# New delays in the planner that orders the work behind attention, and a fixed place for its loads

## The chip, the core and the metric

The kernel runs on one core of one Trainium2 chip. The metric is the device time in microseconds (us); lower is better. Three runs of the kernel before gave 654.6, 655.8 and 655.89 us, so the median is 655.8 us. TensorE is called PE here, VectorE DVE, ScalarE ACT, GpSimd POOL, and SyncE SP; PEld is PE's loading of weights.

## The reference

Three layers follow one another on 1152 tokens (2 batches of 576) of 512 channels:

```python
scores = 0.125 * q @ k.T + slope[h] * -abs(i - j)      # 8 heads of 64, window of 128, causal
x = softmax(scores) @ v                                # to (1152, 512)
p = probs / (probs.sum(-1) + 1e-9)                     # 4 experts
x = sum(p[:, e:e+1] * (relu(x @ w1[e]) @ w2[e]) for e in range(4))      # w1 512x1024
xn = x / sqrt(mean(x * x) + 1e-6) * rms_g
out = (silu(xn @ w_gate) * (xn @ w_val)) @ w_out       # 512x1536 and back
```

## The kernel before, in words

Every fp32 operand of a product is split in two fp32r parts, a high part (a copy on ACT) and a low part (a subtraction on DVE), and three matmuls stand for one. The experts are taken in 8 units of half an expert (u = 0 to 7), the last layer in 3 units of 512 hidden channels. In a unit the first products (into the hidden channels) use a scheme with seven products of half-size blocks in place of eight (`products`, L1057): tokens and weights are first added and subtracted in blocks on DVE, and the seven results are joined by a chain of small steps. One call of `products` gives PE seven blocks of six matmuls each, into banks a and c or b and d by turns: pa, pb, pc and pd, and then, adding to the first ones, ka, kc and kd. Behind pa ACT copies the bank to `x`; behind pb DVE adds into `x`; behind pc it adds to the first half of `r`, behind pd again. kc may start when the first add to `r` is done, since it writes the bank which that add reads, and kd when the second is. Behind kd come two more adds, and then relu, or silu and a multiplication, into `h` (L1142, L1148, L1154). The second products (`out_plain`, L1198) go over 9 tiles of 128 tokens with 12 matmuls of 512 columns each (L1207); their left side is the split of `h` (tile `oa`, made by `plain_parts`, L1178), their right side the split of the second weights (tile `wa`).

Besides this, DVE and ACT do side work all the time: the splits and block sums of the next unit's weights (`raw` to `wb` and `wa`), and a conversion of the last layer's weights from 64-bit words (`converted`, L985: ACT at L1014, DVE at L1017, L1020, L1023, in tile `stage`), which SP stores to DRAM (L1032) and loads again later. The loads of raw weights go into a ring of two buffers (`raw`), those of 64-bit words into a ring of three (`scratch`, named t in the code), both at L865.

Attention is a list written out by hand (`ORDERS`, `Flow`). Behind it a planner sets the order, when the program is built:

- `Plan.pe` takes PE's blocks in program order and keeps PE's clock `self.t`. `Plan.now` (L138) issues a step that the products need. `Plan.later` puts side work on a list with a time by which it is due. `Plan.step` (L92) picks from the list what can start soonest, with 0.03 per us of due time added, and `now` calls it to fill the time until the needed step is ready. With `slack`, `now` takes first what is due within it.
- A step's cost is `HOLD + elements * RATE`: it holds DVE for 0.07 + n/960 us, ACT for 0.09 + n/1200, and a load of n = 512 holds the queue for 1.48. Its result counts as there `MORE` later (DVE 0.085, ACT 0.1, a load 2.0, PE 0.17). `End.seen` says when an engine may use it: `LAT` = 0.04 later on another engine, and on the same engine already when the hold ends.
- A side step is taken into the time ahead of a needed one when it ends at most 0.18 us behind it.

At the end (L1534 to L1544) each engine's instructions are tied one to the next in this order, from the first of attention on; SP's only as far as attention goes (`listed`). SP's later loads and stores are ordered by the framework's own scheduler, which may put them between attention's.

Of the kernel before, what the change touches and what calls it, by code (L numbers as in the profile page):

```python
# [42 lines left out]
class End:  # L43
# [10 lines left out]
    def seen(self, e):  # L54

        if self.of is not None:
            return max((x.seen(e) for x in self.of), default=0.0)
        return self.hold if e == self.e and e is not None else self.own + Plan.LAT


class Plan:

    LAT = 0.04
    HOLD = {"d": 0.07, "a": 0.09, "q": 0.2}
    MORE = {"d": 0.085, "a": 0.1, "q": 2.0, "t": 0.17}
    RATE = {"d": 1 / 960, "a": 1 / 1200, "q": 0.0025}

    def __init__(self, free):  # L70
# [21 lines left out]
    def step(self, until, only=None, due=None):  # L92

        found = None
        for i, job in enumerate(self.jobs):
            if due is not None and job[4] > due:
                continue
            b = self.best(job)
            if b and b[0] < until and (only is None or b[1] == only and (due is not None or b[0] + self.cost(only, job[1]) < until + 0.18)):
                key = (b[0] + 0.03 * job[4], job[4], i)  # L100
                if found is None or key < found[0]:
                    found = key, job, b[1]
        if found is None:
            return False
        _, job, e = found
        self.jobs.remove(job)
        needs = job[2]
        if job[6]:
            ring, done = job[6]
            used = min(ring, key=lambda x: x.t)  # L110
            ring.remove(used)
            ring.append(done)
            done.slot = used.slot
            needs = needs + [used]
        self.issue(e, job[1], needs, job[3], job[5])
        return True

    def issue(self, e, n, needs, emit, end):
        start = max(self.free[e], self.ready(needs, e))
        emit(e)  # L120
        self.free[e] = start + self.cost(e, n)
        end.own, end.e, end.hold = self.free[e] + self.MORE[e], e, self.free[e]

# [29 lines left out]
    def pe(self, n, cols, needs, emit):  # L153
# [4 lines left out]
        self.t = start + n * (cols / 2400 + 0.013)  # L158
        return End(self.t + self.MORE["t"], "t", self.t)


class Flow:
# [4 lines left out]
    FORM = {"s": "s", "o": "o", "z": "o", "x": "x"}  # L167
    LAT = {"t": 0.055, "d": 0.036, "a": 0.036, "p": 0.17, "q": 0.1}

# [10 lines left out]
    def run(self, orders, shared):  # L180
# [14 lines left out]
        while any(rows.values()):  # L195
            heads = [(e, r[0]) for e, r in rows.items() if r and all(n in done for n in self.ops[r[0]][3])]
            for e, i in heads:
                kind, _, costs, needs, _ = self.ops[i]
                t = max([self.free[e]] + [done[n] + self.LAT[e] for n in needs if at[n] != e or e == "q"])
                if e == "t":  # L200
# [35 lines left out]
def tile_fused(ctx: ExitStack, tc: tile.TileContext, qS, kS, vS, probs, w1, w2, wgv, wo, g, out):  # L236
# [123 lines left out]
    with (  # L360
# [37 lines left out]
        mark = len(tc.nc.cur_bb.bb.instructions)  # L398
# [354 lines left out]
        prev = dict.fromkeys("sxowf")  # L753
# [31 lines left out]
        listed = len(tc.nc.cur_bb.bb.instructions)  # L785
# [4 lines left out]
    more_slot = End(0.0)  # L790
# [8 lines left out]
    pl = Plan(flow.free)  # L799
# [3 lines left out]
    coming, gates, outs = [], [], []  # L803
# [38 lines left out]
    class Issued:  # L842
# [5 lines left out]
        @property  # L848
        def t(self):
            return self.end.t - Plan.MORE["q"] - pl.LAT  # L850

        def seen(self, e):
            return self.end.t - Plan.MORE["q"]

# [87 lines left out]
    def load_one(src, due, slots=None):  # L942

        slots = slots or [take("wa") for _ in range(4)]
        return load_unit(*src, 0, slots, slots, due)
# [232 lines left out]
    def plain_parts(t, due):  # L1178

        na, da = take("oa")  # L1180

        def w(p):
            return na.slot[:, p, :].rearrange("p (k m) -> p k m", k=4)

        gs = groups(t, t + 1)
        src = h[:, :, t * P : (t + 1) * P]
        end = parts_of(512, w, lambda: src, [na] + [written[g] for g in gs], due)
        for g in gs:
            reading[g].append(end)
        copied[t] = end  # L1190
        return w, end, da
# [24 lines left out]
    def out_tiles(w, put, parts, ahead, between=lambda t: None, last=(), width=DM, tiles=(0, NTT), begun={}):  # L1216

        for t in range(*tiles):
            for i in range(t, min(t + ahead + 1, tiles[1])):
                if i not in parts:  # L1220
                    parts[i] = plain_parts(i, pl.t + 2.7 * (i - t))
            end = t == NTT - 1
            out_plain(parts.pop(t), w, t, put, last if end else (), width if end else DM, t > tiles[1] - 3, begun.get(t))
            between(t)
# [47 lines left out]
    units = [f(20 + 10 * i) for i, f in enumerate(load_w1(*W1[1]))]  # L1272
    right = [first, token_sums(1, End(0.0), w1_read, 28)[0]]
    rewrite(1)
    for t0 in (S, S + HT):
# [5 lines left out]
        if t0 == S:  # L1281
            parts = {t: plain_parts(t, pl.t + 2 + t - 4) for t in (4, 5)}
# [121 lines left out]
    for u in range(1, NU):  # L1404
        w, w_read = nxt
        now_units, units = units, []
        parts = {}
        last = u == NU - 1

        def put(t, c, src, needs, u=u):  # L1410
            return mix(u, t, c, src, needs)

        if last:
            hg = pl.later("q", 256, [], lambda e: nc.sync.dma_start(out=g_cols, in_=g.rearrange("(k p) -> p k", p=P)), pl.t)
        for i, gr in ((0, 0), (1, 0), (0, 1), (1, 1)):
            hidden_products(now_units[i], right[gr], i, gr)
            if (i, gr) == (0, 1) and not last:
                more = load_w1(*W1[u + 1])
                units.append(more[0](pl.t + 20))
            elif (i, gr) == (0, 1):  # L1420
                more = load_w1(*gates[1:3])
                units.append(more[0](pl.t + 18))
                out_tiles(w, put, parts, 1, finish, tiles=(0, 4))
            if (u, i, gr) == (1, 0, 1):
                store_next(3, pl.t)
            if (i, gr) == (1, 0):
                if last:
                    pl.later("a", 1500, [], lambda e: nc.scalar.activation(out=rstd, in_=ident[:, :NTT], func=AF.Sqrt), pl.t)
                for t in range(2 if last else 3):
                    parts[t] = plain_parts(t, pl.t + 6 + 2 * t)  # L1430
        if not last:
            units.append(more[1](pl.t + 20))
            nxt = load_w2(W2[u + 1], pl.t + 30)
            store_next(STORES[u], pl.t + 24)
            spare = KEEP * (u == NU - 2)
            out_tiles(w, put, parts, 3, last=w_read, tiles=(0, NTT - spare))
            kept = [(t, parts.get(t) or plain_parts(t, pl.t)) for t in range(NTT - spare, NTT)], w, w_read
            if u == NU - 2:
                lent = [take("t") for _ in range(RINGS["t"])]
                for x, done in lent:  # L1440
                    i = thirds.index(x.slot)
                    x.slot = late(lambda i=i: third(i, [P, 2, 512], F32R))
                    done.slot = late(lambda i=i: third(i, [P, 1024], F32))
                first_units = [load_one(gates[0], pl.t + 20, [*lent, (more_slot, End())])]
            continue
        first_units += units
        first_units.append(more[1](pl.t + 18))
        begun, tags = {}, (("a", "c"), ("b", "d"))[(turn["pr"] + 1) % 2]
        for i in range(4, TA):
            parts[i] = plain_parts(i, pl.t - 4)  # L1450
        for n, (t, x) in enumerate(kept[0]):
            begun[t] = out_first(x, kept[1], tags[n // 2], kept[2] if t == NTT - 1 else ())
            if n == 1:
                transposes(pl.t + 6, 0, 1, 2, 3)
                out_tiles(w, put, parts, 0, finish, tiles=(4, TA))
        units = [load_one(gates[3], pl.t + 20)]

        def between(t):
            finish(t)
            if t == NTT - KEEP:  # L1460
                transposes(pl.t + 2, *range(4, TA))
                sums.append(exact_sums(0, pl.t + 2.72 * (NTT - 1 - t)))

        sums = []
        out_tiles(w, put, parts, 2, between, w_read, tiles=(TA, NTT), begun=begun)
# [12 lines left out]
    units = [f(start + 52 + 6 * i) for i, f in enumerate(pair)]  # L1478
# [20 lines left out]
    for u in range(NV):  # L1499
        if u == 0:  # L1500
            right, parts = first_unit()
            pl.slack = None
        else:
            parts = {}
# [28 lines left out]
    traced = tc.nc.cur_bb.bb.instructions  # L1533
    ET = mybir.EngineType  # L1534
    for e in (ET.PE, ET.DVE, ET.Activation, ET.Pool, ET.SP):
        prev = None
        for i in traced[mark : listed if e == ET.SP else None]:
            if i.engine == e:
                if prev is not None:
                    tc.add_manual_dep(  # L1540
                        i, prev.name, mybir.DependencyInfo(mybir.DependencyClass.NoSync, mybir.DependencyReason.DATA),
                        reason="order",
                    )
                prev = i  # L1544


# [30 lines left out]
```

## Time and profile before

| | |
|---|---|
| median of 3 runs (lowest to highest) | 655.8 us (654.6 to 655.89) |
| the profiled execution: its time | 654.55 us |
| its span, first to last instruction | 652.8 us |
| granted TensorE clock over the span | 1.00 |
| PE, DVE, ACT, POOL busy in the span | 642.2, 512.7, 323.2, 43.4 us |
| instructions of PE (matmuls) | 4226 |

The span is the time on the core; the 1.75 us between it and the execution's own time lie around it. Busy PE time counts matmuls that overlap, so it hides short stops: a stop is read from the distance between the starts of two matmuls. Attention takes the first 82 us, with the first expert's products filled in, the experts go on to 442 us, and the last layer takes the rest.

### The profile page before, as it was taken

To read this page: it belongs to the slowest core of one execution; us is meant where nothing else is said; L and a number is where in the kernel's file an instruction comes from. 1 tells how busy PE (TensorE), PEld (TensorE's weight loads), DVE (VectorE), ACT (ScalarE), POOL (GpSimd) and SP (SyncE) were. 2 spreads that over 40 slices of the span, in tenths; PEclk is the share of its full clock that TensorE was granted. 3 is DMA by queue.
4 is the path that set the end of the run, shared out by engine and by line. 5 is a ranking of instruction groups with operands and counts; after the bars stand their busy time and mean duration, and the time that the engine had idled before them with its cause. 6 is when DMAs were issued, how large, how long until landed. Compare 5 with 4: busy or idle time off the path is not lost.

```text
span 652.8 us, 11281 instructions
## 1 busy us (share of the span) xinstructions
PE 642.2 (98%) x4226; PEld 579.2 (89%) x4226; DVE 512.7 (79%) x1167; ACT 323.2 (50%) x756; POOL 43.4 (7%) x94
## 2 busy tenths in 40 slices
PE   6999998999999999999999999999999999999998
PEld 5688797989989989989889898889998999899986
DVE  6988676697786987987978988798989488838573
ACT  6988464543542642633534456676446334303230
POOL 6764100000000000000000000000000000000000
PEclk9999999999999999999999999999999999999999
DMA  8542014056133635545435231101314300101012
GB/s 280 179 143 66 1 34 135 26 178 188 57 97 129 194 97 154 169 125 150 144 130 175 79 102 50 33 32 66 101 63 162 114 30 35 34 2 40 27 49 96
DMA packets 24758, 64.71 MB, mean 99 GB/s; under 512 B 3200, under 2 KB 6272, under 8 KB 24704
## 3 DMA queue, kind: packets, MB, share of 16 engines
q1 hardware_dynamic: 24416, 63.70, 30.7%
q8 instruction: 33, 0.54, 0.3%
q10 hardware_dynamic: 288, 0.30, 0.1%
q14 instruction: 21, 0.17, 0.1%
HBM read 52.19 MB, written 11.80 MB: 98 GB/s over the span
## 4 chain that ended last, share of the span: by engine, by line
PE 88%; DVE 6%; ACT 2%; DMA 2%; issue 1%; SPq 0%; DVEq 0%
PE ps_c L1075 12%; PE ps_a L1207 12%; PE ps_d L1075 11%; PE ps_b L1207 9%; PE ps_a L1075 8%; PE ps_b L1075 8%; PE ps_d L1207 8%; PE ps_c L1207 7%; PE a L673 2%; PE pst L570 2%; PE po L589 2%; PE a L704 2%; PE s L503 2%; DVE wb L821 1%; DVE r L824 1%
## 5 line engine op out<-in xcount | busy, mean ns | idle before, releaser
L1207 PE MATMUL ps_a<-wa,oa 128*128 128x512 f32 (+1 forms) x372 | 85.0, 382 | 0.0
L1207 PEld LDWEIGHTS ps_a<-wa,oa 128*128 128x128 f32 x372 | 68.3, 188 | 13.6
L828 ACT ACTIVATE wb<-raw 128x512 fp32r<-128x512 f32 (+1 forms) x99 | 50.3, 531 | 50.6 <-DVE raw L821 46.1
L821 DVE TENSOR_TENSOR oa<-h,oa 128x512 fp32r<-128x512 f32 x95 | 64.0, 683 | 2.3 <-ACT oa L828 2.0
L1207 PE MATMUL ps_b<-wa,oa 128*128 128x512 f32 x276 | 65.0, 390 | 0.0
L828 ACT ACTIVATE oa<-h 128x512 fp32r<-128x512 f32 x95 | 56.0, 619 | 8.7 <-DVE h L1154 4.5
L1207 PEld LDWEIGHTS ps_b<-wa,oa 128*128 128x128 f32 x276 | 51.2, 188 | 10.2
L1207 PE MATMUL ps_d<-wa,oa 128*128 128x512 f32 x240 | 56.2, 389 | 0.0
L821 DVE TENSOR_TENSOR wb<-raw,wb 128x512 fp32r<-128x512 f32 (+1 forms) x99 | 54.2, 566 | 0.1
L1207 PEld LDWEIGHTS ps_d<-wa,oa 128*128 128x128 f32 x240 | 45.0, 188 | 9.3
L1207 PE MATMUL ps_c<-wa,oa 128*128 128x512 f32 x216 | 50.7, 389 | 0.0
L828 ACT ACTIVATE wa<-raw 128x512 fp32r<-128x512 f32 (+1 forms) x55 | 30.3, 590 | 38.1 <-DMA raw<-in_w 26.4
L1207 PEld LDWEIGHTS ps_c<-wa,oa 128*128 128x128 f32 x216 | 40.5, 188 | 8.3
L1075 PE MATMUL ps_d<-xh,wb 128*128 128x288 f32 (+2 forms) x176 | 43.5, 300 | 2.1 <-DVE r L824 2.1
L821 DVE TENSOR_TENSOR wa<-raw,wa 128x512 fp32r<-128x512 f32 (+1 forms) x55 | 34.1, 642 | 13.7 <-ACT wa L828 13.7
L1075 PE MATMUL ps_b<-xh,wb 128*128 128x288 f32 (+2 forms) x176 | 43.0, 298 | 0.0
L1075 PE MATMUL ps_c<-xh,wb 128*128 128x288 f32 (+2 forms) x176 | 41.8, 295 | 0.0
L1075 PE MATMUL ps_a<-xh,wb 128*128 128x288 f32 (+2 forms) x176 | 41.1, 291 | 0.0
L1142 ACT ACTIVATE h<-r 128x576 f32<-128x576 f32 x28 | 19.2, 686 | 40.0 <-DVE r L824 40.0
L824 DVE TENSOR_TENSOR r<-ps_c,x 128x288 f32<-128x288 f32 (+2 forms) x52 | 23.2, 446 | 16.6 <-PE ps_c L1075 13.8
L828 ACT ACTIVATE x<-ps_b 128x288 f32<-128x288 f32 (+2 forms) x26 | 10.6, 408 | 47.5 <-PE ps_b L1075 47.4
L821 DVE TENSOR_TENSOR raw<-raw 128x256 f32<-128x256 f32 x78 | 32.9, 422 | 1.5
(290 smaller groups left out, 1559.4 us busy)
## 6 DMA issues: line engine op xcount, KB each, us to landing
raw<-in_w SPq DMA_DIRECT2D x32, 512.0 KB, 3.8
scratch<-in_wgv SPq DMA_DIRECT2D x24, 512.0 KB, 4.6
f<-stage SPq DMA_DIRECT2D x36, 256.0 KB, 2.6
raw<-f SPq DMA_DIRECT2D x18, 512.0 KB, 3.3
scratch<-in_wo SPq DMA_DIRECT2D x12, 512.0 KB, 4.6
vt<-in_vS SPq DMA_DIRECT2D x4, 512.0 KB, 6.3
out_y<-acc SPq DMA_DIRECT2D x8, 256.0 KB, 2.0
qt<-in_qS SPq DMA_DIRECT2D x7, 288.0 KB, 4.2
```

The costliest lines, as they stand in the source:

```text
L503: nc.tensor.matmul(sps[n, t][o : o + D, :], lhsT=qts[n][rows, t * D : (t + 1) * D], rhs=kts[n][rows, k0:k1], start=True, stop=True,)
L570: nc.tensor.transpose(pst[:w, j, :], tts[n % 2][:, 2 * kb + j, c0 : c0 + w], ident)
L589: nc.tensor.matmul(po[r, kb * P : kb * P + len(range(blocks.shape[1])) * P], lhsT=vt[:, kb, v], rhs=blocks[:, :, 1:3, :] if j else blocks[ ...
L673: nc.tensor.matmul(box[0], lhsT=a, rhs=x[:, k, tok], start=k == 0 and a is wh and x is xh, stop=k == 3 and a is wl)
L704: nc.tensor.matmul(box[0], lhsT=tile[0][:, x, k, :], rhs=v[:, i, :], start=k == 0 and x == i == 0, stop=k == 3 and x == 1)
L821: EN[e].tensor_tensor(out=out, in0=a, in1=b, op=ALU.subtract)
L824: EN[e].tensor_tensor(out=out, in0=a, in1=b, op=ALU.add)
L828: nc.scalar.activation(out=out, in_=a, func=AF.Copy)
L1075: nc.tensor.matmul(ps, lhsT=s[:, k, :], rhs=t(k), start=start and m == 0, stop=m == 5, skip_group_check=True,)
L1142: return wrote(gr, pl.now("a", tok.stop - tok.start, needs + was_reading[gr], lambda e: nc.scalar.activation(out=h[:, c, tok], in_=src, fu ...
L1207: nc.tensor.matmul(ps[:, :width], lhsT=a(s)[:, k, :], rhs=w[k][0]()[:, i, c], start=not (n or begun), stop=(n == 11))
```

## The change

The times of the planner change, some due times with them, and the tie of SP's instructions. Nothing that is computed changes.

```diff
     def seen(self, e):
-        return self.hold if e == self.e and e is not None else self.own + Plan.LAT
+        return self.own + (Plan.LAT if e != "t" else 0.0 if self.e == "t" else Plan.PELAT)
 class Plan:
-    LAT = 0.04
+    LAT, PELAT = 0.08, 0.15
     HOLD = {"d": 0.07, "a": 0.09, "q": 0.2}
-    MORE = {"d": 0.085, "a": 0.1, "q": 2.0, "t": 0.17}
+    MORE = {"d": 0.085, "a": 0.1, "q": 3.0, "t": 0.17}
...
-            if b and ... (due is not None or b[0] + self.cost(only, job[1]) < until + 0.18)):
+            if b and ... (due is not None or b[0] + self.cost(only, job[1]) < until + 0.0)):
...
     def out_tiles(...):
-                    parts[i] = plain_parts(i, pl.t + 2.7 * (i - t))
+                    parts[i] = plain_parts(i, pl.t + 2.7 * (i - t) - 4)
...
                 more = load_w1(*gates[1:3])
-                units.append(more[0](pl.t + 18))
+                units.append(more[0](pl.t + 30))
...
-                first_units = [load_one(gates[0], pl.t + 20, [*lent, (more_slot, End())])]
+                first_units = [load_one(gates[0], pl.t + 50, [*lent, (more_slot, End())])]
...
-        first_units.append(more[1](pl.t + 18))
+        first_units.append(more[1](pl.t + 30))
...
     for e in (ET.PE, ET.DVE, ET.Activation, ET.Pool, ET.SP):
         prev = None
-        for i in traced[mark : listed if e == ET.SP else None]:
+        for n, i in enumerate(traced[mark:], mark):
             if i.engine == e:
                 if prev is not None:
                     tc.add_manual_dep(i, prev.name, ...)
-                prev = i
+                if e != ET.SP or n < listed:
+                    prev = i
```

In words: a result counts for any engine, its own too, only when it is wholly written, plus 0.08 us (plus 0.15 for PE, which keeps its own order). A load is taken to land 3.0 us behind its hold, not 2.0. A side step must end before the needed step can start. The splits of `h` for a second product are due 4 us earlier, the first two weight units of the last layer later. And each of SP's instructions behind attention comes behind attention's last one.

## Rows read from the trace of the kernel before

**Rows 1.** Windows: us, busy time of PE, PEld, DVE, ACT, POOL, clock, DMA share, GB/s

```profile
100.00:125.00 25.00, 23.23 (x158) 22.06 (x158) 14.61 (x30) 10.99 (x22) 0.00 (x0) 1.00 0.32 104
425.00:500.00 75.00, 74.61 (x477) 69.31 (x476) 68.88 (x148) 44.83 (x99) 0.00 (x0) 1.00 0.25 83
```

**Rows 2.** Timeline of PE at 109 us: start, us, what, idle before

```profile
109.08 0.29 PE L1075 MATMUL ps_b<-xh,wb 128*128 128x288 f32 x1
111.15 0.40 PE L1075 MATMUL ps_d<-xh,wb 128*128 128x288 f32 x1 [1.77 <-DVE r L824]
111.39 0.30 PE L1075 MATMUL ps_d<-xl,wb 128*128 128x288 f32 x1
```

**Rows 3.** Chain that ended last, from 100 to 112 us

```profile
103.85 5.50 DMA raw<-in_w
```

**Rows 4.** Timeline of DVE, 104 to 113 us

```profile
107.13 0.46 DVE L824 TENSOR_TENSOR x<-ps_b,x 128x288 f32<-128x288 f32 x1 [2.10 <-PE ps_b L1075]
110.03 0.69 DVE L821 TENSOR_TENSOR wa<-raw,wa 128x512 fp32r<-128x512 f32 x1 [2.45 <-ACT wa L828]
110.64 0.45 DVE L824 TENSOR_TENSOR r<-ps_d,x 128x288 f32<-128x288 f32 x1
```

**Rows 5.** Timeline of PE at 221 and at 363 us

```profile
221.25 0.29 PE L1075 MATMUL ps_a<-xl,wb 128*128 128x288 f32 x1
221.38 0.29 PE L1075 MATMUL ps_a<-xh,wb 128*128 128x288 f32 x1
221.66 0.40 PE L1075 MATMUL ps_c<-xh,wb 128*128 128x288 f32 x1
221.90 0.29 PE L1075 MATMUL ps_c<-xl,wb 128*128 128x288 f32 x1
...
222.43 0.29 PE L1075 MATMUL ps_c<-xh,wb 128*128 128x288 f32 x1
222.63 0.66 PE L1075 MATMUL ps_c<-t,wb 128*128 128x288 f32 x3
...
363.16 0.40 PE L1075 MATMUL ps_c<-xh,wb 128*128 128x288 f32 x1
```

**Rows 6.** Timeline of DVE, 216 to 222 us

```profile
218.67 0.45 DVE L824 TENSOR_TENSOR r<-ps_d,x 128x288 f32<-128x288 f32 x1
...
220.59 0.45 DVE L824 TENSOR_TENSOR x<-ps_a,x 128x288 f32<-128x288 f32 x1
221.15 0.46 DVE L824 TENSOR_TENSOR r<-ps_c,x 128x288 f32<-128x288 f32 x1
221.52 0.68 DVE L1023 SCALAR_TENSOR_TENSOR stage<-scratch,stage 128x512 int32<-128x512 int32 x1
222.12 0.45 DVE L824 TENSOR_TENSOR r<-ps_c,r 128x288 f32<-128x288 f32 x1
```

**Rows 7.** Timeline of PE at 457 and at 601 us

```profile
456.93 0.31 PE L1075 MATMUL ps_b<-xh,wb 128*128 128x320 f32 x1
457.53 0.41 PE L1075 MATMUL ps_d<-xh,wb 128*128 128x320 f32 x1 [0.30 <-DVE r L824]
...
600.62 0.28 PE L1075 MATMUL ps_a<-xh,wa 128*128 128x256 f32 x1
601.05 0.39 PE L1075 MATMUL ps_c<-xh,wa 128*128 128x256 f32 x1
```

**Rows 8.** Timeline of SP, the first 40 us

```profile
3.66 0.56 SPq L865 DMA_DIRECT2D scratch<-in_wgv  x1
...
6.90 0.43 SPq L1414 DMA_DIRECT2D g_cols<-in_g  x1
...
37.05 0.51 SPq L430 DMA_DIRECT2D vt<-in_vS  x1
```

**Rows 9.** Everything that PE waited for (us, times, longest)

```profile
...
PE ps_d L1075 <- DVE r L824: 2.1, 2, 1.8
PE s L503 <- DMA kt<-in_kS: 1.7, 1, 1.7
```

More of the change, by code (lines that the diff above doesn't have):

```diff
@@ L98, in step @@
             b = self.best(job)
-            if b and b[0] < until and (only is None or b[1] == only and (due is not None or b[0] + self.cost(only, job[1]) < until + 0.18)):
+            if b and b[0] < until and (only is None or b[1] == only and (due is not None or b[0] + self.cost(only, job[1]) < until + 0.0)):
                 key = (b[0] + 0.03 * job[4], job[4], i)
```

## The prediction

> **What bounds the kernel now.** I read the page's busy times first: PE is at work in 642.2 of 652.8 us, so no other engine can set the time except by stopping PE. The windows say where to look: from 100 to 125 us PE lacks 1.8 us, and from 425 to 500 us it lacks 0.4, while DVE there works 68.88 of 75 us and has 6.1 us to spare [rows 1]. Busy time hides short stops, since matmuls overlap, so I then went through PE's timeline and looked only at the distance between starts. Undisturbed, matmuls of 288 columns start 0.13 us apart from 221.25 to 221.38 [rows 5]. What is longer is a stop:
>
> - At 109 us PE starts 2.07 us after the matmul before, and the next one 0.24 later. Less 0.13 each time that is 1.94 + 0.11 = 2.05 us [rows 2].
> - At 221.66, 0.28 less 0.13, and 0.24 less 0.13 behind it; at 222.63 0.20 less 0.13, and three matmuls there take 0.66 where 2 x 0.13 + 0.29 = 0.55 would do. That is 0.15 + 0.11 + 0.07 + 0.11 = 0.44 us. It returns in each of four units of the experts, 4 in all, the last at 363.16: 1.76 us [rows 5].
> - At 457.53, 0.60 against 0.15 (320 columns), and at 601.05, 0.43 against 0.12 (256 columns) [rows 7]: 0.45 and 0.31, each with the 0.11 behind it that every stop has: 0.98 us.
>
> Together that is 4.8 us; smaller ones are left out. Everything else behind attention is matmul after matmul. So this change, which leaves PE's work alone, can win some 4.8 us there and hardly more.
>
> What ends each stop? PE waits for the adds into `r` [rows 2, 7, 9]. At 109 us a load issued at 103.85 took 5.50 us to land [rows 3]. ACT's copy for `wa` waited for it, DVE's subtraction for `wa` waited at 110.03 for the copy, and the add into `r`, which PE needs, stood in DVE's queue behind the subtraction until 110.64 [rows 4]. Its own inputs were there long before: pc's matmuls ended 12 matmuls ahead of 109.08, at about 107.5, and the add into `x` had started at 107.13. At 221 us nothing is loaded: a chain of adds, `x` at 220.59, `r` at 221.15, `r` at 222.12 with a conversion step at 221.52 put between, is simply later than planned [rows 6].
>
> **The planner's clock against the trace.** The add at 220.59 lasts 0.45 us and the one that needs its result starts 0.56 behind it; the step at 221.52, which needs nothing of it, follows after only 0.37 [rows 6]. The old plan gives both 0.07 + 288/960 = 0.37. The new one keeps 0.37 for the independent step and plans 0.37 + 0.085 + 0.08 = 0.535 for the dependent one, within 0.03 of the trace. For PE behind a DVE add the trace has 221.66 - 221.15 = 0.51, plus the 0.11 that follows, 0.62; the old plan says 0.37 + 0.085 + 0.04 = 0.495, the new one 0.37 + 0.085 + 0.15 = 0.605. For the load, old 1.48 + 2.0 = 3.48, new 4.48, trace 5.50 [rows 3]. So each new number moves toward the rows and none passes them. One rule speaks against it: the Trainium skill, VectorE: DVE Perf Modes, section The DRAIN you can't avoid, says that the next DVE step never starts before the pipe is empty, so that a dependence costs nothing on top; by it the extra 0.165 is fiction. Rows 6 go against that rule here, with 0.37 and 0.56; what it would give is a rival below.
>
> **The change part by part.**
>
> Loads at 3.0: the planned landing moves 1.0 us later, with two latencies 0.08 more. The old plan put the subtraction for `wa` ahead of an add that could start at about 107.9 (a latency after pc's end), so it expected it before then; 1.08 us later it falls behind that add, and most likely behind the second add too, which could start some 0.8 us after the first (one block of six matmuls, 6 x 0.13). The copy still stands in ACT's queue and waits, but behind it is only relu's copy of a bank that PE needs a product later. Bounds for this term: 2.05 when both adds go ahead, 1.0 when only the wait gets shorter. I take **2.05**, since the first add alone lets PE's kc go on and the second needs only 0.8 us.
>
> Dependent steps at full length, and no side step that overruns: in the chain of rows 6 the step at 221.52 would have to end before the add at 222.12 can start. Each link is worth 0.165 to 0.2 of lateness, and 0.18 was the permitted overrun; a stop of 0.44 is about two links. Which side step comes there in the new order can't be read from the rows, so I take three of the four stops as gone, **1.3 us**; bounds 0 and 1.76.
>
> The same at 457 and 601 us, where DVE is 92% busy (68.88 of 75) around the first [rows 1]: half, **0.5 us**; bounds 0 and 0.98.
>
> Due times: splits of `h` 4 us earlier, two weight units 12 us later, one 30 later. No row shows a wait for either, so nothing is gained; the cost, if a split now pushes a needed step, is one stop like those at 221 us, **0.44 us**, bounds 0 and the slower rival.
>
> SP's order: two loads leave the start, words for `scratch` at 3.66 and `g_cols` at 6.90, and go behind 37.05 [rows 8]. They are moved past attention's loads of q, k, v and the first weights. PE's one wait for a load in attention is for `kt` [rows 9], which is ahead of both in the queue; so I cost it at nothing. The cover is that attention waits for DVE, not for loads; if it is gone the other way, the loads behind them come sooner, at most that one wait of 1.7 us, which I don't count. DVE, ACT and PE keep attention's order, since the planner starts behind it.
>
> **The sum:** 2.05 + 1.3 + 0.5 - 0.44 = 3.4 us. The profiled execution of 654.55 us would become 651.15; it lies 1.25 under the median, so against the median of 655.8 the forecast is **652.4 us**.
>
> **The rivals.**
>
> Only the load's term: a dependent step costs no more than any other (the page's rule), or the stops at 221 us come from work that must be done there. Then the reordering moves nothing else: 655.8 - 2.05 = 653.75. For it: that term alone rests on a plain error of the plan; against it, 0.37 and 0.56. Chance 0.14, of which 0.04 for the rule.
>
> No change: every order is new, and the stops come back elsewhere, since a load can still take 5.50 where 4.48 is planned: 655.8. Chance 0.13.
>
> Slower: late weights in the last layer. Side steps are refused that would not wholly fit, and their dependents are held longer, so DVE leaves holes. Around 425 to 500 us it has 6.1 us left [rows 1]. Once the refused work there exceeds this, weights whose due time was moved back are not split when a unit of the last layer begins, and PE waits. The nearest price is its one wait for a late load, 2.05 us [rows 2]; at the start of each of three units that is 6.15, against 2.05 + 1.3 won elsewhere: 655.8 + 2.8 = 658.6. Against it: the chip already pays these latencies, so the holes exist today and the same work fits. Chance 0.11.
>
> **How the numbers follow.** The forecast has 0.62. Within it the terms' bounds run from all 4.8 us gone, 651.0, to little more than the load's. The low end goes 0.8 lower, to 650.2, for the smaller stops and because one run before lay 1.2 under the median. The high end, 656.2, takes in the case without change and leaves out the slower one. About 0.2% (1.3 us) is what a measurement of this kernel tells from no change. The forecast and the load's term alone both lie under it: 0.76 faster. Same is 0.13, slower 0.11.
>
> **What would show it.** In the profile after: no stop of 2 us near 109, and the add into `r` ahead of the `wa` subtraction there; four starts fewer or shorter at the third block of the experts' late products; starts of dependent adds still 0.56 apart; `scratch` and `g_cols` behind the last `vt`; attention's end unmoved. I am wrong if PE shows new stops, above all with a wait for `wb` or `wa` at a unit's start in the last layer, or if DVE's busy time there falls while weights come late.

## The result, and the profile after

The changed kernel takes 648.06 us (median of 4 runs, 647.76 to 648.33) against 655.68 us (4 runs, 654.6 to 655.89): a ratio of 0.9887, 95% interval 0.987 to 0.9904. That is 7.6 us faster, more than twice the 3.4 us forecast, and below the range given (650.2 to 656.2).

| | before | after |
|---|---|---|
| profiled execution: time | 654.55 | 647.98 |
| its span | 652.8 | 646.2 |
| PE's stops behind 80 us, added up | 6.87 | 2.16 |
| start of PE's scores for the third pair of heads | 12.56 | 10.72 |

The third line is worked out from PE's timeline: for any two matmuls in sequence from 80 us on, the distance between their starts less (columns/2400 + 0.013) us, all added. In each kernel 1.2 us of it is no stop but the 36 transposes, which are that much longer.

So the 6.57 us between the two profiled executions have two parts: 4.7 us of stops behind attention are gone, and in attention PE starts the third pair of heads 1.84 us sooner, a lead that stays the same up to 100 us. The medians differ by 1.1 us more. Of 50 further runs of the kernel before, made beside the experiments below, 19 had a granted clock of 1.000 over the span, as its profiled execution and all four runs of after had (median 654.42 us), and 29 had 0.997 (median 655.88); what that is stands in the last section.

First the windows of after that answer to [rows 1]; the columns are the same.

```profile
100.00:125.00 25.00, 25.00 (x179) 24.40 (x178) 16.72 (x35) 13.13 (x27) 0.00 (x0) 1.00 0.31 106
425.00:500.00 75.00, 74.92 (x479) 69.76 (x478) 69.39 (x147) 46.22 (x102) 0.00 (x0) 1.00 0.27 94
```

PE now works all of the first window, and DVE in the second does 0.5 us more, not less (the same stretch of time, by then 5 to 6 us further on in the work): no sign of the holes that the slower rival feared from refused side steps.

PE's timeline at the place of [rows 2], and DVE's for [rows 4]:

```profile
107.25 0.29 PE L1075 MATMUL ps_b<-xh,wb 128*128 128x288 f32 x1
107.38 0.29 PE L1075 MATMUL ps_d<-xh,wb 128*128 128x288 f32 x1
107.51 0.30 PE L1075 MATMUL ps_d<-xl,wb 128*128 128x288 f32 x1
```

```profile
105.29 0.46 DVE L824 TENSOR_TENSOR x<-ps_b,x 128x288 f32<-128x288 f32 x1 [1.08 <-PE ps_b L1075]
105.99 0.46 DVE L824 TENSOR_TENSOR r<-ps_d,x 128x288 f32<-128x288 f32 x1 [0.24 <-PE ps_d L1075]
106.79 0.46 DVE L824 TENSOR_TENSOR r<-ps_d,r 128x288 f32<-128x288 f32 x1 [0.34 <-PE ps_d L1075]
109.15 0.69 DVE L821 TENSOR_TENSOR wa<-raw,wa 128x512 fp32r<-128x512 f32 x1 [1.90 <-ACT wa L828]
```

Both adds into `r` now stand ahead of the subtraction for `wa`. The load still lands late (the subtraction waits 1.90 us for the copy of it), but no add that PE needs stands behind it. The one larger stop of after lies at 441 us, where before has none, 0.39 less 0.15 and then 0.26 less 0.15:

```profile
440.94 0.31 PE L1075 MATMUL ps_a<-xh,wb 128*128 128x320 f32 x1
...
441.33 0.42 PE L1075 MATMUL ps_a<-th,wb 128*128 128x320 f32 x1
441.59 0.31 PE L1075 MATMUL ps_a<-tl,wb 128*128 128x320 f32 x1
```

Now the start, which I had costed at nothing. SP's queue of after, which answers to [rows 8]: the words and `g_cols` come behind the last `vt`, as the diff says.

```profile
35.21 0.73 SPq L430 DMA_DIRECT2D vt<-in_vS  x1
35.98 0.58 SPq L865 DMA_DIRECT2D scratch<-in_wgv  x1
36.61 0.54 SPq L1414 DMA_DIRECT2D g_cols<-in_g  x1
```

PE's start with the third pair and the DVE step of that time, of the kernel before and then of after:

```profile
12.03 0.16 DVE L546 TENSOR_SCALAR st<-st 128x3 f32<-128x3 f32 x1
...
12.56 0.34 PE L503 MATMUL s<-kt,qt 64*64 64x64 f32 x4 [2.21 <-DVE st L546]
```

```profile
11.93 0.16 DVE L546 TENSOR_SCALAR st<-st 128x3 f32<-128x3 f32 x1
...
10.72 0.50 PE L503 MATMUL s<-kt,qt 64*64 64x64 f32 x10 [0.56 <-DMA kt<-in_kS]
```

The profile of before names DVE's step as what PE waited for. In after the same step runs at nearly the same time, 11.93, and PE starts 1.2 us ahead of it. So PE never needed that step; what it waited for was the load of `kt`. The name is an inference, the last of several semaphores to rise, and it was wrong here. The time from issue to landing says the same. In before this `kt` is issued at 6.42, behind the words, and takes 6.0 us (line 424 from 6.3 to 6.8 us), so it lands at 12.43; after's chain of work has it at 6.54 with 4.05 us, landing at 10.59. In both PE starts 0.13 us behind the landing.

```profile
DMA to landing us min/median/max: 6.0/6.0/6.0
```

```profile
6.54 4.05 DMA kt<-in_kS
```

Of the 1.84 us, 0.50 are there one pair earlier, at the second pair's scores, before and then after:

```profile
7.72 0.82 PE L503 MATMUL s<-kt,qt 64*64 64x64 f32 x18 [1.72 <-DMA kt<-in_kS]
```

```profile
7.22 0.82 PE L503 MATMUL s<-kt,qt 64*64 64x64 f32 x18 [1.18 <-DMA kt<-in_kS]
```

That `kt` is issued at 2.10, ahead of the words, and still takes 5.49 us with them behind it and 4.98 in after. The seven profiles with both loads in the start have 5.22 to 6.00 us for it, five without the words (after, e1, e7, e9, e12) 4.44 to 5.16.

### The profile page after: what moved, and what is told of

Read it like the earlier page. It is cut to its first block, busy times and chain, and to the rows that moved or that the text cites. A ratio compares the mean times of both kernels' runs of the same rounds, so it can differ in the third digit from the quotient of the medians.

```text
span 646.2 us, 11270 instructions
## 1 busy us (share of the span) xinstructions
PE 640.0 (99%) x4226; PEld 578.9 (90%) x4226; DVE 513.7 (79%) x1165; ACT 325.0 (50%) x764; POOL 43.4 (7%) x94
## 4 chain that ended last, share of the span: by engine, by line
PE 96%; ACT 2%; DVE 1%; DMA 1%; issue 0%; SPq 0%
PE ps_d L1075 13%; PE ps_a L1207 13%; PE ps_c L1075 12%; PE ps_b L1075 9%; PE ps_b L1207 9%; PE ps_a L1075 9%; PE ps_c L1207 8%; PE ps_d L1207 8%; PE a L673 2%; PE pst L570 2%; PE po L589 2%; PE a L704 2%; PE s L503 2%; PE ps_b L1235 1%; PE ps_d L1235 1%; DMA kt<-in_kS 1%
## 5 line engine op out<-in xcount | busy, mean ns | idle before, releaser
L824 DVE TENSOR_TENSOR r<-ps_d,x 128x288 f32<-128x288 f32 (+2 forms) x52 | 24.3, 467 | 11.5 <-PE ps_d L1075 9.6
```

The lines of the kernel that those rows point to most:

```text
L824: EN[e].tensor_tensor(out=out, in0=a, in1=b, op=ALU.add)
```

## The experiments

Each ran beside runs of the kernel before, whose medians were 655.1 to 655.8 us.

| run | us | stops behind 80 us | third pair starts at |
|---|---|---|---|
| before, profiled | 654.55 | 6.87 | 12.56 |
| after, profiled | 647.98 | 2.16 | 10.72 |
| e1 before + tie of SP | 652.77 | 7.08 | 10.89 |
| e2 after without the tie | 649.83 | 2.20 | 12.84 |
| e3 before + load 3.0 | 651.04 | 2.83 | 12.71 |
| e4 before + dependents | 651.35 | 2.85 | 12.51 |
| e5 before + no overrun | 653.29 | 5.57 | 12.51 |
| e6 before + due times | 654.85 | 7.01 | 12.62 |
| e7 after, load 2.0 | 648.96 | 2.86 | 10.41 |
| e8 before, load 1.0 | 659.55 | 11.05 | 12.58 |
| e9 after, g_cols free | 648.62 | 3.05 | 10.35 |
| e10 after, words free | 649.44 | 2.23 | 11.93 |
| e11 after, v later | 647.95 | 2.31 | 9.84 |
| e12 after, load 1.0 | 652.33 | 6.44 | 10.77 |

The times of the runs e1 to e12 are medians of 3 to 10 runs, the other two columns come from one profile each.

**The tie, alone and left out.**

```diff
 # e1, on the kernel before
-        for i in traced[mark : listed if e == ET.SP else None]:
+        for n, i in enumerate(traced[mark:], mark):
...
-                prev = i
+                if e != ET.SP or n < listed:
+                    prev = i
 # e2: the reverse, on the kernel after
```

> Before with SP's tie alone. Theory: the load at 3.66 us held up kt of the third pair of heads, and PE's start at 12.56 waited for that load, not for DVE as the view of waits says; then the tie alone moves the start to about 10.7, PE's stops behind attention stay as in the kernel before (4.8 us), and the time is 655.7 - 1.9 = 653.8. Rival: PE waited for DVE there, and the start differs for another reason; then 655.7.

> After with SP's instructions tied as before (the planner's numbers stay new). Theory: the start of attention goes back to 12.56 us, the stops behind attention stay away: 648.1 + 1.9 = 650.0. Rival (the tie is worth nothing): 648.1. Rival (the stops behind attention went away because of the tie): above 652.

The tie alone gives 0.9966 (0.9949 to 0.9983) of before's time. PE starts the third pair at 10.89, and at 109 us it stops as before:

```profile
10.89 0.34 PE L503 MATMUL s<-kt,qt 64*64 64x64 f32 x5 [0.34 <-DVE st L523]
...
107.42 0.29 PE L1075 MATMUL ps_b<-xh,wb 128*128 128x288 f32 x1
109.68 0.40 PE L1075 MATMUL ps_d<-xh,wb 128*128 128x288 f32 x1 [1.96 <-DVE r L824]
```

Without it the start falls back, while the stops stay away. This profile says what the start waits for:

```profile
12.84 0.46 PE L503 MATMUL s<-kt,qt 64*64 64x64 f32 x7 [0.34 <-DMA kt<-in_kS]
```

Both times came out within 1.1 us of the theory, and the rivals fall: the tie is worth some 2 us, all of them in attention's first 13 us, and it removes no stop behind attention.

**Which of the two loads.**

```diff
 # e9 and e10, on the kernel after; early holds one instruction's name
-            if i.engine == e:
+            if i.engine == e and i.name not in early:
```

> After, with only g_cols (2 KB in 512 packets of 4 bytes) free to go into attention's loads again; the words stay behind. Theory (the 512 KB of words made the wait): PE starts the third pair's scores at about 10.8 us, 648.1. Rival (the many small packets made it): at about 12.5 us, 650.

> After, with only the first load of words (512 KB) free to go into attention's loads again; g_cols stays behind. Theory: PE starts the third pair's scores at about 12.5 us again, 648.1 + 1.9 = 650.0, and with PE idle twice some runs show a granted clock under 1.000. Rival: the same as after, 648.1.

```profile
3.69 0.53 SPq L1415 DMA_DIRECT2D g_cols<-in_g  x1
...
10.35 0.50 PE L503 MATMUL s<-kt,qt 64*64 64x64 f32 x10 [0.16 <-DVE st L523]
```

```profile
3.65 0.58 SPq L866 DMA_DIRECT2D scratch<-in_wgv  x1
...
11.93 0.34 PE L503 MATMUL s<-kt,qt 64*64 64x64 f32 x4 [1.39 <-DMA kt<-in_kS]
```

The first is e9, the second e10. With `g_cols` at the start PE is not late; with the 512 KB of words there it waits 1.39 us for `kt`. So the words make most of it. They took back 1.2 of the 1.84 us in this one profile, not all. The seven profiles with both loads in the start lie between 12.51 and 12.84, so 11.93 is outside their spread; whether the rest is `g_cols` on top of the words is not shown by one profile. The `kt` issued at 2.10 took 4.77 us in e10, so the words alone are not shown to delay a load ahead of them. In e9 a stop of 0.56 us came at 112 us that after's profile does not have; it is taken up below.

**The planner's numbers, one by one.**

```diff
 # e3
-    MORE = {"d": 0.085, "a": 0.1, "q": 2.0, "t": 0.17}
+    MORE = {"d": 0.085, "a": 0.1, "q": 3.0, "t": 0.17}
 # e4
-        return self.hold if e == self.e and e is not None else self.own + Plan.LAT
+        return self.own + (Plan.LAT if e != "t" else 0.0 if self.e == "t" else Plan.PELAT)
-    LAT = 0.04
+    LAT, PELAT = 0.08, 0.15
 # e5: until + 0.18 becomes until + 0.0;  e6: the four changed due times
```

> Before with a load planned to land 3.0 us behind its hold instead of 2.0, nothing else. Theory: the stop of 2.05 us at 109 us goes, the four of 0.44 and those at 457 and 601 stay: 655.7 - 2.0 = 653.7. Rival: the stop only shrinks by the 1.0 that the plan moves: 654.7. Rival: the other stops come from the same number: 651.

> Before with results counted as there only when wholly written, on the same engine too (LAT 0.08, PELAT 0.15), nothing else. Theory: the four stops of 0.44 and those at 457 and 601 go, the one at 109 stays: 655.7 - 2.7 = 653.0. Rival: this alone removes the stop at 109 too, since the order on DVE flips anyhow: 651.0. Rival: it is the permitted overrun that makes the small stops, and they stay: 655.7.

> Before with the permitted overrun of a side step at 0 instead of 0.18 us, nothing else. Theory (latencies left out of the plan make the stops, not the overrun): the stop of 2.05 us at 109 us stays, the small ones shrink by at most half: 654 to 655. Rival (the overrun makes the small stops): they go, 655.1 - 2.7 = 652.4.

> Before with the changed due times alone. Theory: they change what is done early, not what the plan knows of latencies, so the stops behind attention stay within 1 us of 4.8, 655. Rival: earlier splits of h relieve DVE where the products need it, 653 or less.

I expected e3 and e4 to share the stops between them. Each took nearly all: 6.87 us fell to 2.83 and to 2.85, and the times to 0.993 (0.991 to 0.995) and 0.9939 (0.9916 to 0.9961). In both a rival came true. In e3 the four stops at 221 us and its like are gone; two stops, at 456 and 483 us, are left, of which this is the larger:

```profile
455.06 0.31 PE L1075 MATMUL ps_b<-xh,wb 128*128 128x320 f32 x1
455.68 0.41 PE L1075 MATMUL ps_d<-xh,wb 128*128 128x320 f32 x1 [0.30 <-DVE r L824]
```

That the four stops hang on the number for DMAs too can be read from ACT's timeline, which the prediction did not read at that place. Before, at 217 us, and e3, at 220 us:

```profile
217.45 0.68 ACT L1014 ACTIVATE stage<-scratch 128x512 f32<-128x512 f32 x1 [0.68 <-DMA f<-stage]
```

```profile
219.67 0.39 ACT L828 ACTIVATE x<-ps_a 128x288 f32<-128x288 f32 x1
219.96 0.66 ACT L1014 ACTIVATE stage<-scratch 128x512 f32<-128x512 f32 x1
```

The conversion waited 0.68 us for a store to free its buffer, and the number for a load's landing is the number for a store's too. With 3.0 the planner puts the conversion behind the copy to `x` that the products need, and it waits for nothing. That this wait alone made the stops is a reading of the rows, not shown apart.

The overrun (e5, 0.9972, 0.9957 to 0.9988) leaves the stop at 109 us and the four behind it and removes those from 457 us on, 1.3 us in all and more than expected; the due times (e6, 1.0002, 0.9987 to 1.0018) win nothing.

**Is it truth, or only another order?** Since any one edit reorders hundreds of steps, the order before might just have been unlucky. So the load's number was moved the wrong way, on both kernels, and moved back on after.

```diff
 # e8, on the kernel before
-    MORE = {"d": 0.085, "a": 0.1, "q": 2.0, "t": 0.17}
+    MORE = {"d": 0.085, "a": 0.1, "q": 1.0, "t": 0.17}
 # e12, on the kernel after: 3.0 becomes 1.0;  e7: 3.0 becomes 2.0
```

> Before with the planner's number for a load moved the wrong way: landing 1.0 us behind its hold instead of 2.0. This leaves PE's work and DVE's order of needed steps alone and makes the plan less true. Theory (a truer clock is what helps): PE's stops behind attention are as large as before or larger, 4.8 us or more, so 655 or above; the stop at 109 us stays. Rival (the order before was merely an unlucky draw, and any other order does as well): stops behind attention under 2.5 us, about 651.

> After with a load planned to land 1.0 us behind its hold. Theory: with the plan wrong by more than 2 us on loads, copies and subtractions stand in the queues in front of steps that PE needs; stops of 4 us or more in all come back behind attention: 652 or above. Rival (true times of dependents protect the order): under 650.

> After with a load planned to land 2.0 us behind its hold, as before. Theory (the load's number and the dependents' times each make the order true enough by themselves, as the two runs with one of them alone showed): at most 1 us more than after, 648.1 to 649.1. Rival (the load's number is needed): the stop of 2 us at 107 us returns, 650.1.

| a load lands behind its hold after | 1.0 | 2.0 | 3.0 |
|---|---|---|---|
| other numbers as before | 659.55 | 655.1 | 651.04 |
| other numbers as after | 652.33 | 648.96 | 648.06 |

The 655.1 is the median of before's runs beside e3. The medians were not all taken side by side, so the ratios to before decide. In the upper row both steps are clear: e8 is slower than before, 1.0064 (1.0039 to 1.0088), and e3 faster. In the lower row the step from 1.0 to 2.0 is clear, 0.9958 (0.9941 to 0.9976) against 0.9891 (0.9875 to 0.9908); the one from 2.0 to 3.0 is not, since after has 0.9887 (0.987 to 0.9904). The stop of e8 at the place of 109 us has grown to 2.9 us, and the waits behind it are those of [rows 3, 4]. PE, and then ACT:

```profile
111.26 0.29 PE L1075 MATMUL ps_d<-xh,wb 128*128 128x288 f32 x1
114.25 0.42 PE L1075 MATMUL ps_d<-th,wb 128*128 128x288 f32 x1 [2.70 <-DVE r L824]
114.48 0.42 PE L1075 MATMUL ps_d<-tl,wb 128*128 128x288 f32 x1
...
112.47 1.15 ACT L828 ACTIVATE wa<-raw 128x512 fp32r<-128x512 f32 x2 [4.19 <-DMA raw<-in_w]
```

So a load planned to land sooner than it does costs time. The stop at 109 us follows the number: it is gone with 3.0 and has grown with 1.0. The lower row shows that longer times of dependents make the order less sensitive, but do not make up for a load planned much too short: e12, with 1.0, has the stop at this place again, 2.35 us long.

```profile
107.28 0.29 PE L1075 MATMUL ps_b<-xh,wb 128*128 128x288 f32 x1
109.77 0.40 PE L1075 MATMUL ps_d<-xh,wb 128*128 128x288 f32 x1 [2.19 <-DVE r L824]
```

That the truth of the number is what helps is not shown. The four stops of 0.44 at 221 us and its like are gone in e8 too, where the number moved away from the truth, so for them another order was enough. This is e8 at that place:

```profile
226.10 0.30 PE L1075 MATMUL ps_a<-xh,wb 128*128 128x288 f32 x1
226.24 0.29 PE L1075 MATMUL ps_c<-xh,wb 128*128 128x288 f32 x1
```

The conversion on ACT stands ahead of the copy to `x` there, as in before, but it waits for nothing, which fits the reading above:

```profile
221.17 0.67 ACT L1014 ACTIVATE stage<-scratch 128x512 f32<-128x512 f32 x1
...
224.47 0.39 ACT L828 ACTIVATE x<-ps_a 128x288 f32<-128x288 f32 x1
```

Nor is 3.0 nearer to most of the transfers that it stands for. The page of before gives their size and the median time to landing:

```profile
raw<-in_w SPq DMA_DIRECT2D x32, 512.0 KB, 3.8
scratch<-in_wgv SPq DMA_DIRECT2D x24, 512.0 KB, 4.6
f<-stage SPq DMA_DIRECT2D x36, 256.0 KB, 2.6
raw<-f SPq DMA_DIRECT2D x18, 512.0 KB, 3.3
```

The plan's 3.48 us are nearer to the raw weights, the stores and the weights loaded again than 4.48, which is nearer to the words alone. But of the 79 loads behind 80 us 17 land within 3.48 us and 52 within 4.48. So 3.0 covers the slower loads; whether a still longer number does as well or better was not tried.

A longer number does not protect from every late load. In e9 DVE and ACT have after's order, instruction by instruction, but the loads issued at 103.38 and 103.99 us take 5.80 and 6.46 us (in after 4.82 and 5.52). ACT's copies for `wa` wait for them, the copy to `x` stands behind those, and PE stops for it:

```profile
112.33 0.40 PE L1076 MATMUL ps_a<-xh,wb 128*128 128x288 f32 x1 [0.29 <-ACT x L828]
```

With what follows at 113 us that makes nearly all of the 0.9 us by which e9's stops exceed after's, in one and the same order. e4 and e7 stop at this place too, which is nearly all of the 0.7 us that each has more than after, so that difference is no measure of the numbers left out.

**A step further.** After still waits 1.7 us for `kt` in the view of waits:

```profile
PE s L503 <- DMA kt<-in_kS: 1.7, 2, 1.2
```

```diff
 # e11, on the kernel after, in Flow.run: the first v behind the third pair's q and k
+        first, then = self.behind
+        loads.remove(then)
+        loads.insert(loads.index(first) + 1, then)
         rows["q"] = loads
```

> After with the first load of v (576 KB) queued behind q and k of the third pair of heads, instead of in front. Theory: k of the second pair then has the queue to itself and lands some 0.5 us sooner, k of the third some 1 us sooner, until PE waits for DVE's softmax steps instead; PE starts the third pair's scores at 10.2 to 10.4 instead of 10.7 us and the time falls by 0.3 to 0.5 us, 647.7. Rival: v then lands too late for the first product with it (at 13 us), and the time rises by up to 1 us.

```profile
9.84 1.05 PE L506 MATMUL s<-kt,qt 64*64 64x64 f32 x20
...
12.31 1.52 PE L592 MATMUL po<-pt,vt 128*64 128x256 f32 x12
```

PE starts the third pair at 9.84, 0.88 us sooner, without a wait, and the first product with v is not held up. The span is 645.8 against 646.2 us. The median, 647.95 (647.58 to 649.83), can't be told from after's 648.06: the start has little more to give.

## Why the prediction was wrong, point by point

- **What bounds the kernel**: right. PE's stops were the loss, and the list of them was nearly complete: behind attention it lacks one of 0.36 us at 484 us. It left out attention, on the ground that the planner's order does not reach there.
- **SP's order, "I cost it at nothing"**: this step failed. It was worth 1.84 us in the profiles and about 2.3 us in the median of e1. The reason I gave was that PE's one wait for a load is for a `kt` ahead of both in the queue. The costly wait, at 12.56 us, is for the next `kt`, issued at 6.42 behind the words. I read it as one for DVE, as the view of waits names it, and so took the load behind which `kt` stood for harmless. Of the cover I wrote that "attention waits for DVE, not for loads"; e1, e2 and e10 show that it waited for the load. Nor was the `kt` ahead in the queue untouched: issued at 2.10, it took 0.51 us less in after. The bound I gave, that loads come sooner by at most the wait of 1.7 us, was near the size, but 1.34 of the 1.84 us belong to the other wait, and I counted none of it. The hint was in [rows 8]: 512 KB issued at 3.66, while attention still loads its own q, k and v on that queue.
- **The load's term, 2.05**: right in size and in mechanism. Both adds went ahead of the subtraction, as the rows after show. But the 5.50 us that I held against 3.48 and 4.48 was one of the slowest loads; against the median of 3.8 the new number does pass the rows. That the dependents' times remove the same stop alone (e4) was not foreseen.
- **The small stops, 1.3 and 0.5 of 2.74**: too low. The four gave 1.6 us, those from 457 us on 1.4, more than the bound of 0.98, since the list lacked the one at 484. My reason, the length of dependent steps, is not shown to be the cause: another number for loads and stores removes the four without it, longer (e3) or shorter (e8), and the overrun alone removes those from 457 us on (e5).
- **One new stop, 0.44, and the due times**: the allowance was close; 0.35 us at 441 us is new. The due times are worth nothing (e6), and the profiles of e3 to e6 do not have this stop, so none of the planner's changes brings it alone.
- **The median**: I set the sum against a profiled execution 1.25 us under the median and carried that distance along. It goes with the lower granted clock in many runs of before, which none of after's four runs has: 1.1 us more. The profiles of e2, e3 and e4, with 0.997, show that clock in attention's start; of the unprofiled runs only the mean is known.
- **The rule of the Trainium skill** (VectorE: DVE Perf Modes, The DRAIN you can't avoid), a rival with 0.04: the section says that the next step does not start until the pipe is empty, and that a semaphore cost nothing extra in its measurement. It adds, which the prediction left out, that a next step that is not held starts earlier. Rows 6 fit the addition, with a start 0.37 us into an add of 0.46, and go against a dependence at no cost, with 0.56; behind 80 us of before's profile all 21 adds of 288 columns that read the result of the one just ahead start 0.55 to 0.56 us behind it. e4 is no test of the rule, since it also changes what the plan counts towards other engines, and e3 removes as much without it.
- **Slower through late weights**: no sign of it; DVE is busier around 425 to 500 us.

Together: 4.7 instead of 3.4 us behind attention, 1.84 instead of 0 ahead of it, and 1.1 of clock.

## What to carry to other kernels

A planner that orders work when the program is built should not be given latencies shorter than those the trace shows. For loads the number that covered more of the slow ones did better here, though the median was nearer to a shorter one: a planned 2.48 us to landing gave 659.55 us, 3.48 gave 655.1 and 4.48 gave 651.04. A load planned too short can put a step that waits ahead of one that the bound engine needs. A change of such a number also makes another order, so test it in both directions before calling it truer. Before costing a moved transfer at nothing, check the named releaser of each wait near it against the time at which it really ran; if the waiting engine could start before or long after it, look for a load. And tie the queue of loads as firmly as the engines, since a large early load without a hurry can delay the smaller ones that PE waits for.

## What was not expected of the hardware

The granted TensorE clock can fall to half after PE has stood still. Two stretches of e8, the first with the stop, the second behind it (columns as in [rows 1]):

```profile
111.00:114.00 3.00, 0.55 (x5) 0.32 (x3) 0.87 (x2) 1.45 (x3) 0.00 (x0) 1.00 0.59 240
114.00:118.00 4.00, 3.75 (x16) 3.75 (x17) 1.71 (x4) 1.36 (x3) 0.00 (x0) 0.57 0.40 135
```

PE works 0.55 of 3 us in the first; in the second the clock is 0.57 on average, that is 1.2 GHz for most of it in place of 2.4, and the matmuls at 114.25 and 114.48 start 0.23 us apart, not 0.13. In attention's start it is the same in e3, where PE works 0.67 of the 2 us ahead of the fall:

```profile
10.00:12.00 2.00, 0.67 (x7) 0.43 (x4) 1.97 (x12) 2.00 (x10) 1.45 (x5) 1.00 1.01 273
12.00:14.00 2.00, 1.29 (x22) 1.32 (x26) 1.30 (x8) 0.71 (x4) 1.42 (x5) 0.72 0.95 294
14.00:16.00 2.00, 2.00 (x19) 1.42 (x12) 0.09 (x2) 0.00 (x0) 1.15 (x3) 0.50 1.08 347
```

Over a whole run that shows as 0.997. It goes with 1.5 us more (655.88 - 654.42 in the runs of before) and strikes only some of a kernel's runs. All runs of after and of e9 had 1.000; of e1, which has the tie and still stops for 2 us at 109, two of ten had 0.997, and those were its slowest, 654.07 and 654.48 us. So a wait of PE costs more than its length where the clock falls behind it.
